# A two-batch channel attention with a SiLU feed-forward on one core: one fixed instruction order from the second pair on, the transposed attention in the scores' PSUM bank, other gaps for v's splits

## Chip, cores and metric

The kernel runs on 1 core of one Trainium2 chip. The metric is device time in microseconds (us). Three runs of the kernel before gave 1025.42, 1025.69 and 1026.45 us; the median is 1025.69 us.

## The reference

Two batches of 6016 positions and 256 channels go through an attention between channels, and its output, read as 12032 tokens of 256, through a feed-forward of width 2048.

```python
def _attn_ref(q, k, v, tau):
    qn = q / (np.linalg.norm(q, axis=1, keepdims=True) + 1e-06)
    kn = k / (np.linalg.norm(k, axis=1, keepdims=True) + 1e-06)
    s = kn.transpose(0, 2, 1) @ qn / tau          # 256 x 256 for each batch
    s = s - s.max(-1, keepdims=True)
    a = np.exp(s)
    a /= a.sum(-1, keepdims=True) + 1e-09
    return v @ a

def _moe_ref(x, w_in, w_out):
    h = x @ w_in                                  # 256 -> 2048
    g = h * (1.0 / (1.0 + np.exp(-h)))
    return g @ w_out                              # 2048 -> 256
```

## The kernel before, in words

The attention matrix of a batch is multiplied into `w_in` once (`mix`), so that the feed-forward reads v directly. Every f32 factor is split into two f16 halves ("high" by ScalarE, the remainder "low" by VectorE), and a product is three f16 matmuls. Both big products are arranged as 2 x 2 block products with seven instead of eight multiplications; the sums and differences that this needs are made on VectorE, ScalarE and by accumulating DMAs.

**Pairs and units.** v's columns are cut into 12 pairs (0 to 11) of 1024 columns; pairs 5 and 11, the last of each batch, have 896. Pair 0 goes through `emit_pair_group`; pairs 1 to 11 through `emit_unit`, eight units (0 to 7) each. A full unit takes TensorE about 9.5 us. A unit has four gaps ("slots" 0 to 3), one after each yield of `emit_unit`; work of others is put into them:

- slot 0: the products `y`, `x`, `z` into the PSUM banks of those names; ScalarE copies y and x to `c` (L810, L812); VectorE makes `g<-c,z` (L790). VectorE also runs the remainder of the unit before (`hl<-g,sg,hl`, L803);
- slot 1: `y` and `x` again, ScalarE copies x (L821), VectorE `g<-c,y`, and the second remainder (L803) of the unit before;
- slot 2: `x` (S3 T3), VectorE `g<-x,c`;
- slot 3: `x` (A22 T4), ScalarE Silu `g<-x,alpha` (L793) straight from the bank. The next unit's second product writes this bank again.

The second layer's matmuls (`o<-...`, L913) stand in a list `ready` and fill each slot by a budget.

**v of the next pair** (`scale_v(p + 1)`). A generator scales v to its largest magnitude (four reductions L148 on VectorE, then `pow2_scale`, whose matmul goes through the bank `z`), and then writes the tile `m`: highs on ScalarE (L550, `m<-v_t` or `m<-x`), lows on VectorE (L553), and between them sums (L574, L559). For pair 1 alone the scale comes from a sum of squares on ScalarE. The table `V_PLACES` says in which unit and slot each step is taken; key 0 is for pair 4 and was the default, 1 for pair 5, 2 for pair 6.

**Attention of the second batch.** It is computed while pairs 0 to 4 run (`attention(1)`, its scores in the bank `a`), and ends at pair 5's start: the transposes `tp` (L411) go into the bank `z` (through `small_psum`), and `split` writes `aT` from there (L164 on ScalarE, L165 on VectorE), in two halves. From then on `mix(1, j)` for j = 0 to 7 makes the second batch's `wall` with twelve matmuls `w` each (L443, bank `a`), at the places that the table `MIXES` names by (pair - 4, unit, slot).

**Order.** Within pairs 1 to 11 TensorE, VectorE and ScalarE keep the order in which the program is written (`tc.manual_schedule`); this region is closed and opened again at each pair. Each engine works its list in order, so a waiting instruction holds what stands behind it.

Of the kernel before, what the change touches and what calls it, by code (L numbers as in the profile page):

```python
# [8 lines left out]
F16 = mybir.dt.float16  # L9
F32 = mybir.dt.float32  # L10
# [4 lines left out]
AF = mybir.ActivationFunctionType  # L15
ALU = mybir.AluOpType
AX = mybir.AxisListType
PSUM = bass.MemoryType.PSUM
P = 128
# [11 lines left out]
def channel_attention_then_silu_ffn(ctx, tc, kq, qT, kT, vT, tau, w_in, w_out, outT):  # L31
    nc = tc.nc
    B, N, _, C = kq.shape
    DFF = w_in.shape[1]
    KC = C // P
# [8 lines left out]
    vp = ctx.enter_context(tc.tile_pool(name="vp", bufs=2))  # L44
    hp = ctx.enter_context(tc.tile_pool(name="hp", bufs=1))
    sm = ctx.enter_context(tc.tile_pool(name="sm", bufs=2))
    ps_b = ctx.enter_context(tc.tile_pool(name="ps_b", bufs=1, space=PSUM))
    firsts = {}
# [43 lines left out]
    def small_psum(name):  # L92

        if early[0]:
            return ps_o.tile([P, 512], F32, tag="o", name=name)
        return firsts["z"] if firsts else ps_b.tile([P, 512], F32, tag="z", name=name)
# [175 lines left out]
    def attention(b):  # L272
# [11 lines left out]
        for g, (j, n) in enumerate(groups[min(b, 1)]):  # L284
            if b and g >= 10:
                load_qk(b, g + 3)
            t = staged.pop((b, g))
            if b == 0 and g < 2:
                nc.scalar.activation(out=acc[:, g : g + 1], in_=t[:, :1], func=AF.Square)
            elif b == 0:  # L290
                if j + n == J:
                    nc.vector.tensor_tensor(
                        out=acc[:, 0], in0=acc[:, 0], in1=acc[:, 1], op=ALU.add
                    )
                sq = st.tile([P, 2, 2, C], F32, tag="sq", name="sq", bufs=2)
                nc.scalar.activation(out=sq[:, :n], in_=t[:, :n], func=AF.Square)
                a = acc[:, g % 2 : g % 2 + 1] if g < 4 else acc[:, :n]
# [33 lines left out]
        else:  # L331
            half = sm.tile([P, 2 * KC], F32, tag="half", name="half", bufs=1)
            nc.vector.tensor_scalar(
                out=tot, in0=tot, scalar1=1e-30, scalar2=None, op0=ALU.add
            )
            nc.vector.tensor_scalar(
                out=half.bitcast(U32), in0=tot.bitcast(U32), scalar1=1, scalar2=None,
# [3 lines left out]
                out=half, in0=half, scalar1=SEED, scalar2=None, op0=ALU.mult  # L341
            )
            yield
            for _ in range(2):
# [4 lines left out]
                    out=half, in0=half, scalar1=0.5, scalar2=None, op0=ALU.mult  # L349
# [3 lines left out]
        if b == 0:  # L353
# [6 lines left out]
            out=rn, in0=rn, scalar=2e-6, in1=root, op0=ALU.add, op1=ALU.add  # L360
# [41 lines left out]

        aT = sm.tile([P, 2, KC, C], F16, tag="aT", name="aT", bufs=1)
        if b:
            tp = small_psum("tp")
            tps = [tp[:, cb * C : (cb + 1) * C] for cb in range(KC)]
        else:
            tps = [small_psum("tp")[:, :C] for cb in range(KC)]
        for cb, tp in enumerate(tps):
            for db in range(KC):  # L410
                nc.tensor.transpose(  # L411
                    tp[:, db * P : (db + 1) * P], es[cb][:, db * P : (db + 1) * P], ident
                )
        if b == 0:
            yield
        for cb, tp in enumerate(tps):
            src = tp.rearrange("p (d c) -> p d c", d=KC)
            split(src, *(aT[:, u, :, cb * P : (cb + 1) * P] for u in range(2)), 2.0**TOP)
# [78 lines left out]
    def scale_v(p):  # L497
        b, n, w = pairs[p]
# [24 lines left out]
            yield  # L523
        if p < 2:
            s, inv = yield from pow2_scale(amax, "v", bufs=2, square=p == 1)
        else:
            quarters = [x for kc in range(KC) for x in v[kc]]
            maxima = amax_of(quarters, "av")
            for _ in quarters:
                next(maxima)  # L530
                yield
            next(maxima)
            amax = steps(maxima)
            scale = pow2_scale(amax, "v", bufs=2)
            next(scale)
            yield
# [636 lines left out]
    with at(0):  # L1173
# [41 lines left out]
        next(sqgen)  # L1215
        filler = attention(1)
    V_PLACES = {
# [3 lines left out]
    }  # L1221
    MIXES = {
# [101 lines left out]
    turned_over = [mix(1, j) for j in range(NI)]  # L1324
    fixed = ExitStack()
    for p, (b, n, w) in enumerate(pairs):
        fixed.close()
        if p not in paired:
            firsts.clear()
        if p in paired:  # L1330
            fixed.enter_context(
                tc.manual_schedule(
                    engines={
                        mybir.EngineType.PE, mybir.EngineType.DVE, mybir.EngineType.Activation
                    }
                )
            )
# [3 lines left out]
        for i in range(NI):  # L1341
# [29 lines left out]
            for _ in (emit_unit if p in paired else emit_pair_group)(p, i):  # L1371
                if ahead:
                    behind(start, ahead, {mybir.EngineType.PE})
                    ahead = None
                if p == 0 and i < 2:
                    start = len(traced())
                    prepare()
                    behind(start, anchor, {mybir.EngineType.DVE, mybir.EngineType.Activation})
                take = 2 if p == 0 and i > 2 and len(pending) > 6 - slot else 1
                over = p == len(pairs) - 1 and i == NI - 1  # L1380
                held_over = p == closing and i == NI - 1
                room_left = 12 * take
                if p in paired:
                    room_left = (
                        (8, 12, 12, 0) if over else (8, 8, 12, 16) if held_over else
                        (8, 12, 12, 8) if p == 1 and i == 0 else (8, 12, 16, 8)
                    )[slot]
                queue = ready if p in paired else pending
                while queue and room_left > 0:
                    cost, run = queue.pop(0)  # L1390
                    run()
                    room_left -= cost
                mark()
                if p == 0 and i < NI - 1 and (i, slot) != (1, 1):
                    nextmix = background(nextmix)
                if p in paired:
                    for j in MIXES.get((p - closing, i, slot), ()) if closing else ():
                        background(turned_over[j])
                    places = V_PLACES.get(p - closing if closing else 0, V_PLACES[0])
                    vgen = background(vgen, places[i].count(slot))  # L1400
                elif i >= 1 and vgen is not None:
                    vgen = background(vgen, 2)
                if p == closing and (i, slot) == (3, 1):
                    steps(sqgen)
                    norms["go"] = True
                if filler is not None and b == 0 and (p or i >= 2):
                    if "go" not in norms or p != closing or slot in ATTENTION[i]:
                        filler = background(filler, 1)
                if p in paired and b == 0 and "go" not in norms and slot in SQUARES[i]:
                    sqgen = background(sqgen) or iter(())  # L1410
                if p == 0 and 2 <= i < 5 and slot in (0, 2):
                    wout = background(wout)
                if p == 0 and i >= 5:
                    if i == 5 and slot == 0:
                        wout = spend(wout, 100)
                        summing = prepare_sums()
                    summing = background(summing)
                slot += 1
# [42 lines left out]
```

## Time and profile before

| | |
|---|---|
| median of three runs | 1025.69 us |
| profiled execution, its own time | 1026.73 us |
| its span, first to last instruction | 1025.0 us |
| TensorE busy | 1006.4 us (98%) |
| VectorE busy | 850.5 us (83%) |
| ScalarE busy | 766.8 us (75%) |
| mean granted TensorE clock | 0.995 |

The profiled execution took 1.7 us more than its span and 1.0 us more than the median. In timeline rows the columns are start (us from the span's start), busy us, engine, source line, operation, written tile <- read tiles, shapes, count of merged instructions, and in brackets the idle time before the first of them with what ended it. Matmul ends are modelled.

### The profile page before, as it was taken

Reading aid. Unit: us, or ns where it says so; the run is one execution under the profiler, and the core shown is the slowest. Engines: PE = TensorE matmul, PEld = TensorE weight load, DVE = VectorE, ACT = ScalarE, POOL = GpSimd, SP = SyncE. Lnnn points to the kernel's source line nnn. Section 1 sums busy time; section 2 is a strip of 40 time slices with the busy share of each in tenths; the row PEclk is TensorE's granted clock in tenths of the full one; section 3 lists DMA queues with packets and bytes.
Section 4 is the critical chain, followed back from the end, with each engine's and each line's share of the span. In section 5 each row is a group of like instructions: output and inputs, shape, how many; then the busy total and the mean of one; then the engine's idle time right before and its main releaser. Section 6 shows DMA issues by size and latency. Waiting matters only on the chain.

```text
span 1025.0 us, 20950 instructions
## 1 busy us (share of the span) xinstructions
PE 1006.4 (98%) x8550; PEld 870.2 (85%) x8550; DVE 850.5 (83%) x1339; ACT 766.8 (75%) x1077; POOL 199.5 (19%) x283
## 2 busy tenths in 40 slices
PE   9999999999999999998999999999999999999997
PEld 8877545788888888887998988888888888889997
DVE  6997687688888888897889889889889888888776
ACT  6686797788887887877677867777777777677674
POOL 0011000122212222212122112212122122222231
PEclk9999999999999999999999999999999999999999
DMA  9996010546547547525335244444435435334343
GB/s 368 397 398 201 33 42 1 181 105 202 151 120 210 147 114 211 126 68 159 76 81 139 62 107 105 123 104 122 121 88 140 109 93 144 89 94 112 97 94 85
DMA packets 62036, 138.81 MB, mean 135 GB/s; under 512 B 6642, under 2 KB 20898, under 8 KB 61938
## 3 DMA queue, kind: packets, MB, share of 16 engines
q0 software_dynamic: 30672, 67.98, 28.5%
q1 hardware_dynamic: 30978, 68.95, 19.2%
q8 instruction: 67, 1.10, 0.5%
q10 hardware_dynamic: 288, 0.52, 0.1%
q14 instruction: 31, 0.25, 0.1%
HBM read 57.67 MB, written 12.32 MB: 68 GB/s over the span
## 4 chain that ended last, share of the span: by engine, by line
PE 72%; DVE 11%; ACT 10%; issue 3%; DMA 3%; DVEq 0%; POOL 0%; SPq 0%; ACTq 0%
PE o L913 32%; PE x L783 18%; PE y L783 9%; PE z L783 5%; PE sc L301 4%; ACT g L793 2%; DVE g L790 2%; DVE hl L803 2%; PE o L681 2%; ACT hl L800 2%; PE w L443 1%; DVE m L553 1%; DMA kq_t<-in_kq 1%; DMA raw<-in_w_in 1%; ACT g L729 1%
## 5 line engine op out<-in xcount | busy, mean ns | idle before, releaser
L783 PEld LDWEIGHTS <-wall 128*128 128x128 f16 x3696 | 361.0, 98 | 49.1 <-issue 12.1
L783 PE MATMUL x<-m,wall 128*128 128x256 f16 (+1 forms) x2112 | 283.9, 271 | 4.7 <-DVE g L790 2.2
L803 DVE SCALAR_TENSOR_TENSOR hl<-g,sg,hl 128x1024 f16<-128x1024 f32 (+1 forms) x176 | 221.2, 1257 | 69.3 <-ACT hl L800 68.5
L913 PE MATMUL o<-hl,wo 128*128 128x256 f16 (+1 forms) x2112 | 272.8, 271 | 0.7 <-DVE hl L803 0.7
L913 PEld LDWEIGHTS <-wo 128*128 128x128 f16 x2464 | 240.8, 98 | 24.2 <-issue 1.2
L793 ACT ACTIVATE g<-g,alpha 128x512 f32<-128x512 f32 (+3 forms) x176 | 160.7, 921 | 98.1 <-DVE g L790 97.2
L800 ACT ACTIVATE hl<-g,sg 128x1024 f16<-128x1024 f32 (+1 forms) x176 | 198.1, 1126 | 0.0
L1004 POOL DMA_DIRECT2D sums<-hl x109 | 97.3, 892 | 370.0 <-DMA sums<-hl 125.1
L783 PE MATMUL y<-m,wall 128*128 128x256 f16 (+1 forms) x1056 | 142.8, 272 | 0.1
L821 ACT COPY c<-x 128x512 f32<-128x512 f32 (+1 forms) x88 | 50.7, 577 | 77.4 <-PE x L783 77.2
L913 PE MATMUL o<-t,ws_lo 128*128 128x256 f16 (+1 forms) x398 | 95.3, 271 | 0.0
L913 PE MATMUL o<-t,ws_hi 128*128 128x256 f16 (+1 forms) x398 | 95.2, 271 | 0.0
L790 DVE TENSOR_TENSOR g<-x,c 128x512 f32<-128x512 f32 (+1 forms) x88 | 59.5, 676 | 28.6 <-PE x L783 28.4
L793 ACT ACTIVATE g<-x,alpha 128x512 f32<-128x512 f32 (+1 forms) x88 | 58.8, 668 | 27.0 <-PE x L783 26.4
L997 DVE TENSOR_TENSOR t<-t,hl 128x1024 f16<-128x1024 f16 (+1 forms) x111 | 75.2, 677 | 3.0
L913 PEld LDWEIGHTS <-ws_lo 128*128 128x128 f16 x704 | 69.0, 98 | 6.6
L913 PEld LDWEIGHTS <-ws_hi 128*128 128x128 f16 x704 | 69.0, 98 | 6.6
L301 PE MATMUL sc<-kq_t 128*128 128x256 f32 x320 | 73.8, 381 | 0.6 <-DMA kq_t<-in_kq 0.6
L997 DVE TENSOR_TENSOR t<-hl 128x1024 f16<-128x1024 f16 (+1 forms) x111 | 74.4, 670 | 0.0
L783 PE MATMUL z<-m,wall 128*128 128x256 f16 (+1 forms) x528 | 70.7, 270 | 3.2 <-DVE aT L165 3.2
L790 DVE TENSOR_TENSOR g<-c,y 128x512 f32<-128x512 f32 (+1 forms) x88 | 59.2, 673 | 17.3 <-ACT c L821 16.1
L1002 POOL DMA_DIRECT2D sums<-hl x44 | 31.1, 707 | 204.8 <-DVE hl L803 140.6
(194 smaller groups left out, 1344.1 us busy)
## 6 DMA issues: line engine op xcount, KB each, us to landing
sums<-hl POOLq DMA_DIRECT2D x142, 256.0 KB, 3.3
kq_t<-in_kq SPq DMA_DIRECT2D x39, 512.0 KB, 8.7
sums<-t POOLq DMA_DIRECT2D x54, 256.0 KB, 3.5
extra<-hl POOLq DMA_DIRECT2D x42, 256.0 KB, 3.5
v_t<-in_vT SPq DMA_DIRECT2D x10, 1024.0 KB, 5.5
outT<-sb SPq DMA_DIRECT2D x40, 256.0 KB, 3.6
turned<-in_qT SPq DMA_DIRECT2D x10, 512.0 KB, 6.3
turned<-in_kT SPq DMA_DIRECT2D x10, 512.0 KB, 6.4
```

Of the source, the lines that this page charges most:

```text
L301: nc.tensor.matmul(sc[:, cb, :], t[:, i, 0, cb * P : (cb + 1) * P], t[:, i, 1, :], start=(j + i == 0 and cb == 0), stop=(j + i == J - 1), ...
L681: nc.tensor.matmul(o[:, :h], a[:, f, ee], hl[:, m, :h], start=(c == 1 and i == 0), stop=(c == NF and i == 2),)
L783: nc.tensor.matmul(bank[:, k * wide : (k + 1) * wide], mixed[b, i][:, v, a - 1], m[:, c, x, at : at + wide], start=(first and j + k == 0), ...
L790: nc.vector.tensor_tensor(out=g, in0=a[:, :h], in1=c[:, :h], op=ALU.subtract)
L793: nc.scalar.activation(out=g, in_=src, func=AF.Silu, scale=alpha)
L800: nc.scalar.activation(out=hl[:, :, 0], in_=g, func=AF.Copy, scale=sg)
L803: nc.vector.scalar_tensor_tensor(out=hl[:, :, 1], in0=g, scalar=sg, in1=hl[:, :, 0], op0=ALU.mult, op1=ALU.subtract,)
L821: nc.scalar.copy(c2[:, :h], x[:, :h])
L913: nc.tensor.matmul(o[:, side * wide : (side + 1) * wide], a, x, start=(first and j == 0), stop=(last and j == len(these) - 1), skip_group_ ...
L997: nc.vector.tensor_tensor(out=o, in0=x, in1=y, op=ALU.add)
L1002: nc.gpsimd.dma_start(o, x)
L1004: nc.gpsimd.dma_start(o, y, accum_op=ALU.add)
```

## The change

1. `fixed`, the region of fixed order, is opened once at pair 1 and stays open to the end.
2. For the second batch the transposes `tp` go to a tile of the bank `a`; the step after them is a yield of its own in both batches, so both halves of `aT` are written later and together.
3. `V_PLACES` has new entries: for ordinary pairs the step "low of the first half" moves from unit 5, slot 0 to unit 4, slot 3, and the sum `x<-v_t` from unit 5, slot 1 to unit 5, slot 2; pairs 4, 5 and 6 have their own tables.
4. v of pair 6 (`b and not n`) is scaled by its sum of squares: two Square activations with accumulation on ScalarE and a few one-column VectorE operations in place of four reductions; the pair's `m` is made earlier, as a place for the squares.
5. `MIXES` starts the mixes of the second batch earlier, in unit 3 of pair 5.

```diff
@@ attention
         if b:
-            tp = small_psum("tp")
+            tp = ps_b.tile([P, 512], F32, tag="a", name="tp")
...
-        if b == 0:
-            yield
+        yield
         for cb, tp in enumerate(tps):
@@ scale_v
         if p < 2:
             s, inv = yield from pow2_scale(amax, "v", bufs=2, square=p == 1)
+        elif b and not n:
+            sums = sm.tile([P, KC], F32, tag="av", name="av")
+            m = vp.tile([P, 2, 7, 512], F16, tag="m", name="m")
+            sq = m.rearrange("p a b c -> p (a b c)").bitcast(F32)
+            for kc in range(KC):
+                nc.scalar.activation(
+                    out=sq[:, :w], in_=t[:, kc, :w], func=AF.Square,
+                    accum_out=sums[:, kc : kc + 1],
+                )
+                yield
+            amax = sm.tile([P, 1], F32, tag="av1", name="av1")
+            nc.vector.tensor_tensor(out=amax, in0=sums[:, :1], in1=sums[:, 1:], op=ALU.add)
+            scale = pow2_scale(amax, "v", bufs=2, square=True)
+            next(scale)
+            yield
@@ V_PLACES
-        1: ((2, 3), (0, 2), (2, 3), (0, 1, 2, 3), (0, 2), (2, 3), (0, 1, 2), (1,)),
+        1: ((2,), (2, 3), (0, 1, 2), (0, 2, 2, 2), (0, 0), (3,), (3,), (0, 2)),
@@ the loop over pairs
-        fixed.close()
-        if p not in paired:
-            firsts.clear()
-        if p in paired:
+        if p == 1:
             fixed.enter_context(
```

On ScalarE at the start of pair 5 (line 793 Silu, 550 high of v, 800 high of hl, 810 to 821 copies out of the banks, 164 aT; in the changed kernel the lines are 807, 564, 814, 824 to 835 and 164, and 530 is the Square), before:

```order
L793 ACTIVATE g<-g,alpha 128x512
L550 ACTIVATE m<-x,sv 128x448
L793 ACTIVATE g<-x,alpha 128x512
L800 ACTIVATE hl<-g,sg 128x2x512
L164 ACTIVATE aT<-z 128x2x128
L810 COPY c_5351<-y 128x448
L812 COPY c_5351<-x 128x448
L800 ACTIVATE hl<-g,sg 128x2x512
L164 ACTIVATE aT<-z 128x2x128
L821 COPY c_5394<-x 128x448
```

and in the changed kernel:

```order
L807 ACTIVATE g<-g,alpha 128x512
L807 ACTIVATE g<-x,alpha 128x512
L814 ACTIVATE hl<-g,sg 128x2x512
L564 ACTIVATE m<-x,sv 128x448
L824 COPY c_5336<-y 128x448
L826 COPY c_5336<-x 128x448
L814 ACTIVATE hl<-g,sg 128x2x512
L164 ACTIVATE aT<-tp 128x2x128 x2
L835 COPY c_5380<-x 128x448
L807 ACTIVATE g<-g,alpha 128x2x448
L807 ACTIVATE g<-g,alpha 128x448
L530 ACTIVATE m,av<-v_t 128x1024
```

The last high of pair 5's v went behind the Silu and the first high of hl; the two halves of aT went behind the second high of hl, and a Square came in.

On VectorE in pair 1 (and alike in pairs 2, 3, 4, 6, 7, 8, 9 and 10), from the end of unit 4 to slot 2 of unit 5, before:

```order
L997 TENSOR_TENSOR t_1906<-t_1905,hl 128x1024
L803 SCALAR_TENSOR_TENSOR hl<-g,sg,hl 128x2x512
L645 RECIPROCAL back<-sg 128x1
L646 TENSOR_SCALAR back<-back,iwo 128x1
L790 TENSOR_TENSOR g<-c_2047,z 128x512
L553 SCALAR_TENSOR_TENSOR m<-v_t,sv,m 128x1024
L803 SCALAR_TENSOR_TENSOR hl<-g,sg,hl 128x2x512
L790 TENSOR_TENSOR g<-c_2093,y 128x512
L962 SCALAR_TENSOR_TENSOR sb<-o,back,sb 128x256
L574 TENSOR_TENSOR x<-v_t 128x512
L790 TENSOR_TENSOR g<-x,c_2047 128x512
L997 TENSOR_TENSOR t_2032<-hl 128x1024
```

and in the changed kernel:

```order
L1011 TENSOR_TENSOR t_1906<-t_1905,hl 128x1024
L567 SCALAR_TENSOR_TENSOR m<-v_t,sv,m 128x1024
L817 SCALAR_TENSOR_TENSOR hl<-g,sg,hl 128x2x512
L659 RECIPROCAL back<-sg 128x1
L660 TENSOR_SCALAR back<-back,iwo 128x1
L804 TENSOR_TENSOR g<-c_2048,z 128x512
L817 SCALAR_TENSOR_TENSOR hl<-g,sg,hl 128x2x512
L804 TENSOR_TENSOR g<-c_2093,y 128x512
L976 SCALAR_TENSOR_TENSOR sb<-o,back,sb 128x256
L804 TENSOR_TENSOR g<-x,c_2048 128x512
```

The low of v's first half went ahead of the first remainder of hl, and the sum x<-v_t went behind `g<-x,c` and the two sums t.

On VectorE in unit 6 of pair 5, around `g<-x,c`, before:

```order
L553 SCALAR_TENSOR_TENSOR m<-x,sv,m 128x1024
L803 SCALAR_TENSOR_TENSOR hl<-g,sg,hl 128x2x448
L790 TENSOR_TENSOR g<-c_6177,y 128x448
L473 TENSOR_TENSOR wall<-x,wall 128x896
L559 TENSOR_TENSOR x<-x,v_t 128x512
L790 TENSOR_TENSOR g<-x,c_6114 128x448
L997 TENSOR_TENSOR t_6095<-hl 128x2x448
```

and in the changed kernel (the row ahead of these is the last of three x<-x of a mix, as before):

```order
L817 SCALAR_TENSOR_TENSOR hl<-g,sg,hl 128x2x448
L804 TENSOR_TENSOR g<-c_6166,y 128x448
L804 TENSOR_TENSOR g<-x,c_6104 128x448
L1011 TENSOR_TENSOR t_6085<-hl 128x2x448
L1011 TENSOR_TENSOR t_6085<-t_6085,hl 128x2x448
L1000 TENSOR_TENSOR sb<-sb 128x448
L472 TENSOR_TENSOR wall<-x,wall 128x896
```

A low of v, the remainder `wall` of a mix and a sum of v no longer stand ahead of `g<-x,c`. The list of GpSimd is the same in both kernels; on the SyncE queue one store of pair 5's output now stands ahead of the load of pair 7's v.

## Rows read from the trace of the kernel before

**Rows 1.** The page: busy us, share of the span, instructions of each engine.
```profile
PE 1006.4 (98%) x8550; PEld 870.2 (85%) x8550; DVE 850.5 (83%) x1339; ACT 766.8 (75%) x1077; POOL 199.5 (19%) x283
```

**Rows 2.** Windows: length, then busy us (instructions) of PE, PEld, DVE, ACT, POOL, PEclk, DMA.
```profile
250.00:300.00 50.00, 50.00 (x461) 44.82 (x460) 40.69 (x62) 41.50 (x61) 10.73 (x15) 1.00 0.60 173
...
485.00:490.00 5.00, 5.00 (x34) 4.03 (x34) 2.25 (x5) 0.53 (x1) 0.79 (x1) 0.66 0.31 54
...
550.00:555.00 5.00, 4.44 (x30) 3.81 (x29) 4.03 (x8) 4.39 (x8) 0.73 (x1) 0.66 0.86 277
```

**Rows 3.** Timeline of TensorE: pair 5, unit 0, and the first product of unit 1.
```profile
479.54 0.74 PE L783 MATMUL y<-m,wall 128*128 128x224 f16 x6
481.01 0.73 PE L783 MATMUL x<-m,wall 128*128 128x224 f16 x6 [0.74 <-ACT g L793]
484.96 0.73 PE L783 MATMUL z<-m,wall 128*128 128x224 f16 x6 [3.21 <-DVE aT L165]
...
494.30 0.74 PE L783 MATMUL y<-m,wall 128*128 128x224 f16 x6
```

**Rows 4.** Timeline of ScalarE, same place.
```profile
479.74 0.65 ACT L550 ACTIVATE m<-x,sv 128x448 f16<-128x448 f32 x1
480.30 0.67 ACT L793 ACTIVATE g<-x,alpha 128x512 f32<-128x512 f32 x1
480.87 1.14 ACT L800 ACTIVATE hl<-g,sg 128x1024 f16<-128x1024 f32 x1
```

**Rows 5.** Timeline of VectorE, same place.
```profile
480.42 0.69 DVE L553 SCALAR_TENSOR_TENSOR m<-x,sv,m 128x448 f16<-128x448 f32 x1 [2.45 <-ACT m L550]
...
482.04 1.28 DVE L803 SCALAR_TENSOR_TENSOR hl<-g,sg,hl 128x1024 f16<-128x1024 f32 x1 [0.74 <-ACT hl L800]
...
484.48 0.42 DVE L165 SCALAR_TENSOR_TENSOR aT<-z,aT 128x256 f16<-128x256 f32 x1 [0.83 <-ACT aT L164]
...
485.73 0.62 DVE L790 TENSOR_TENSOR g<-c,z 128x448 f32<-128x448 f32 x1 [0.82 <-PE z L783]
```

**Rows 6.** Timeline of TensorE in pair 1, unit 5, slot 2, to unit 6, slot 0.
```profile
229.09 1.04 PE L913 MATMUL o<-hl,wo 128*128 128x256 f16 x8
230.24 0.81 PE L783 MATMUL x<-m,wall 128*128 128x256 f16 x6
...
231.76 0.82 PE L783 MATMUL y<-m,wall 128*128 128x256 f16 x6
232.67 0.81 PE L783 MATMUL x<-m,wall 128*128 128x256 f16 x6
```

**Rows 7.** Timeline of VectorE in the same unit.
```profile
223.40 1.28 DVE L803 SCALAR_TENSOR_TENSOR hl<-g,sg,hl 128x1024 f16<-128x1024 f32 x1 [0.98 <-ACT hl L800]
...
225.51 1.28 DVE L553 SCALAR_TENSOR_TENSOR m<-v_t,sv,m 128x1024 f16<-128x1024 f32 x1
...
229.49 0.69 DVE L790 TENSOR_TENSOR g<-x,c 128x512 f32<-128x512 f32 x1
```

**Rows 8.** Timeline of ScalarE: the high whose low Rows 7 show at 225.51.
```profile
220.62 1.13 ACT L550 ACTIVATE m<-v_t,sv 128x1024 f16<-128x1024 f32 x1
```

**Rows 9.** Timeline of TensorE: the same product x in pairs 4 and 6.
```profile
458.36 0.82 PE L783 MATMUL x<-m,wall 128*128 128x256 f16 x6 [0.37 <-DVE g L790]
...
621.74 0.81 PE L783 MATMUL x<-m,wall 128*128 128x256 f16 x6 [0.40 <-DVE g L790]
```

**Rows 10.** Timeline of TensorE in pair 5, unit 6.
```profile
547.90 0.83 PE L913 MATMUL o<-hl,wo 128*128 128x224 f16 x7 [0.71 <-DVE hl L803]
...
550.56 1.02 PE L783 MATMUL x<-m,wall 128*128 128x224 f16 x6 [1.45 <-DVE g L790]
```

**Rows 11.** Timeline of VectorE in the same unit.
```profile
548.29 1.09 DVE L473 TENSOR_TENSOR wall<-x,wall 128x896 f16<-128x896 f32 x1
549.29 0.69 DVE L559 TENSOR_TENSOR x<-x,v_t 128x512 f32<-128x512 f32 x1
```

**Rows 12.** Line 266, the Squares of q and k: count, ns min/median/max, first and last start.
```profile
L266 ACT ACTIVATE sq<-turned x24: 934/1042/1049, 193.1 to 433.4; 128x1024 f32<-128x1024 f32 x20, 128x896 f32<-128x896 f32 x4
```

More of the change, by code (lines that the diff above doesn't have):

```diff
@@ L1398, in channel_attention_then_silu_ffn @@
                         background(turned_over[j])
-                    places = V_PLACES.get(p - closing if closing else 0, V_PLACES[0])
+                    places = V_PLACES.get(p - closing if closing else None, V_PLACES[None])
                     vgen = background(vgen, places[i].count(slot))
```

12 rows, old and new, of tables (MIXES, V_PLACES) are left out of this document.

## Prediction

> **What bounds the kernel now.** I read the page's busy shares first, then windows, then the timeline of TensorE for every start that comes late, and last the engines named in the brackets. TensorE is busy 98% of the span, the next engine 83% [rows 1]. From pair 1 on it hardly rests: 50.00 of 50.00 us in a stretch that also holds the step from pair 1 to pair 2, 461 matmuls, so 0.1085 us for 256 columns and by columns 0.095 us for 224 [rows 2]. The change neither adds nor removes a matmul, so it can give back only what TensorE loses by waiting, and a lower clock behind a wait. I count a loss as the start of a matmul minus the start of the row before it plus its matmuls' time. The reader is to see three kinds:
>
> (a) Pair 5, unit 0. y starts at 479.54 and should be issued by 480.11, x starts at 481.01: 0.90 lost. x should be issued by 481.58, z starts at 484.96: 3.38 lost [rows 3]. (A bracket shows 0.17 less than this, because matmul ends are modelled; I add 0.17 where I use a bracket alone.) Then the granted clock is 0.66 over 485 to 490 [rows 2]: of its two levels the lower, 1.2 GHz, for 5 x 0.34 / 0.5 = 3.4 us, which costs half of that, 1.7 us. Sum 6.0 us. As a test: from the y of unit 0 to the y of unit 1, 14.76 us [rows 3], stand 42 matmuls of 224 and 44 of 256 columns, 8.8 us of work; 6.0 are lost.
>
> (b) Pair 5, unit 6. Two waits for VectorE, 0.71 + 0.17 and 1.45 + 0.17 [rows 10], together 2.5, and behind them again 0.66 over 5 us [rows 2], 1.7 us. Sum 4.2 us.
>
> (c) One place in each ordinary pair. At the end of unit 5 x waits for VectorE's `g<-x,c`: 230.24 against 229.09 + 8 x 0.1085, 0.28 lost; then the next unit's x, 232.67 against 231.76 + 6 x 0.1085, 0.26 lost, because the Silu that frees its bank came late [rows 6]. Pairs 2, 3, 7, 8 and 9 repeat this pattern; pairs 4 and 6 lose 0.37 + 0.17 and 0.40 + 0.17 at the first x [rows 9] and, I take it, 0.26 at the second. 6 x 0.54 + 0.80 + 0.83 = 4.9 us. Pair 10 shows no such wait before the first x.
>
> Together 15.1 us; of the few us of other late starts the change touches none.
>
> **The change, part by part.**
>
> *The bank of tp.* z waits because tp lies in its bank until both halves of aT are read; VectorE's part alone came 0.83 late behind ScalarE [rows 3, 5]. In the bank `a` nobody needs it before the first mix, three units later. This removes the 3.38 us. What is late next is x, which waits for the Silu `g<-x`. The new order puts that ahead of the high of v, so it starts at 479.74 instead of 480.30 [rows 4]; x at 480.45, 0.34 late in place of 0.90.
>
> *The price on VectorE.* The high of v now stands behind the Silu and a high of hl: it starts near 479.74 + 0.57 + 1.05 = 481.4 (their busy times less 0.1 of overlap, [rows 4]) and ends at 482.0. VectorE's low waits for it as it did before (2.45 us idle, [rows 5]), now until 482.05. Queued behind it are hl 1.28, `g<-c,z` 0.62, aT twice 0.42, hl 1.28, `g<-c,y` 0.62 [rows 5], two pairs of one-column operations (0.6, my estimate) and `g<-x,c` (0.62), with the low 0.69 in all 6.6 us; neighbours overlap by 0.09 (548.29 + 1.09 against 549.29, [rows 11]), nine times, so VectorE is through at about 488.0. TensorE has 36 matmuls of each width, 7.3 us, and the 0.34 before it needs that: 487.2, so 0.8 lost. The Silu in front of the next unit's x then waits for that one and for the first Square (1.04 and a read-out, [rows 12]) and ends near 490.5; x could start at 490.0: 0.5 lost. With rounding of the overlaps I take 1.8 us of new loss. Bounds: 0.34 if VectorE is early by a microsecond, and 3.5 if each of the three waits is twice as long. (a) gives back 6.0 - 1.8 = 4.2 us.
>
> *The clock.* [rows 2, 3] show the lower level right behind waits of 0.90 and 3.38 us, [rows 2, 10] behind 0.88 and 1.62; behind a lone 0.54 at 458.36 [rows 9] no stretch I read shows it. I leave 0.8 and 0.5, below both, so I count no fall. The Trainium skill (TensorE: Matmul & The Clock Gate, "HAM oscillation — how this bites in real kernels") says that idle between bursts of matmuls takes the array to half clock. By that rule the waits that I leave could call it again, and the time would be that of the first rival.
>
> *The squares.* They take four reductions off VectorE in units 0 to 2 and put two Squares of 1.04 us on ScalarE; 24 such Squares already ran between Silus [rows 12]. The first is priced above; the second, in unit 1, lies in ScalarE's idle time ahead of a Silu that waits for x anyway. Cover gone, it costs at most its own 1.2 us.
>
> *Steps and mixes moved in pair 5.* In unit 6 a low of v (1.2 us with overlap, by the 1024-wide low of [rows 7]) no longer stands ahead of the hl that TensorE waited 0.88 for, and beside it a `wall` (1.00) and a sum (0.60) no longer ahead of `g<-x,c` [rows 11], which comes 2.8 us earlier where 1.62 were missing [rows 10]. Both waits go, 0.3 us to spare at each. The moved work lands behind `g<-x,c` in units 3, 4 and 6, some 2.9 us in one unit, where VectorE then starts the next remainder 1 to 2 us late and has caught up by the next `g<-x,c`; the mixes' 1.3 us on TensorE widen just those units. Price 0, bounds 0 and the old 4.2. The load of pair 7's v goes behind one store; nobody reads that v before unit 2 of pair 6.
>
> *Ordinary pairs.* The low (1.20) moves into the 0.98 us in which VectorE waited for ScalarE before hl [rows 7]. Its high ends at 220.62 + 1.13 = 221.75 [rows 8], VectorE is free at 223.40 - 0.98 = 222.42, so it does not wait; hl starts 0.3 later, and nothing on TensorE needs it in that slot. From there on VectorE is 1.2 - 0.3 = 0.9 early, and without the sum (0.6) `g<-x,c` at 229.49 could run 1.5 earlier, that is as soon as its product is there; 0.28 were missing. The sum lands behind it, in front of stores only. All 4.9 us come back; bounds 0 and 4.9.
>
> *One fixed order.* At the pairs' borders the lists stand as before, and TensorE does not wait there [rows 2]: 0 from both sides.
>
> Sum: 4.2 + 4.2 + 4.9 = 13.3 us. The profiled execution would take 1026.73 - 13.3 = 1013.4; it stands 1.04 above the median, so the median after is 1025.69 - 13.3 = **1012.4 us**.
>
> **The rivals.**
>
> 1. The clock falls once more in pair 5. For it: the waits that I leave stand 2 us apart. Against it: they are shorter than those that were followed by a fall. 1012.4 + 1.7 = 1014.1 us.
> 2. VectorE's queue in units 5 to 7 only moves: `wall`, three x and a sum now follow each other behind `g<-x,c`, and the next hl is late by more than TensorE's matmuls cover. Then (b) stays: 1012.4 + 4.2 = 1016.6 us.
> 3. The low ahead of hl gives the late start to hl and `g<-c,z`, and (c) stays: 1012.4 + 4.9 = 1017.3 us.
> 4. Slower. The low stands ahead of hl, so VectorE now stands still if ScalarE's high is late, with hl, `g<-c,z`, hl, `g<-c,y` and `g<-x,c` queued behind. It has waited 2.45 us for just such a high [rows 5]. A wait of that size in nine pairs puts `g<-x,c` 2.45 later than the 228.4 I expect, with its 0.7 at 231.5 against 229.96: 1.5 lost each, 13.9 in nine, and (c) is not gained: 1012.4 + 4.9 + 13.9 = 1031 us. It decides from the point where the high ends some 2.5 us later than in [rows 8]: then nine losses of 0.9 eat the other gains. Against it: 0.67 us to spare.
> 5. The change does not do what it says (another wait holds z, the lists were never what was late): 1025.7 us.
>
> **How the numbers follow.** Forecast 0.66, rival 1 0.13, rival 2 0.06, rival 3 0.06, rival 4 0.05, rival 5 0.04. Without any new loss the time would be 1025.69 - 15.1 = 1010.6; from there to rival 2 and a little beyond, 1010.5 to 1017.0, lie the forecast and the first two rivals, 0.85. A measurement of this kernel can tell about 0.2%, 2 us. Faster by more: the forecast and rivals 1 to 3, 0.91; same: rival 5, 0.04; slower: rival 4, 0.05.
>
> **What would show it.** In the profile after, z of pair 5's unit 0 follows x within 0.1 us; the window behind it has clock 1.00; TensorE waits there twice for `g<-x`, under 1 us each, once with VectorE's `g<-x,c` as releaser. In unit 6 of pair 5 no wait over 0.3 us stands, and the window has clock 1.00. In ordinary pairs the x at the end of unit 5 starts 0.87 us behind the hl row before it, and VectorE's low shows no wait for ScalarE. I would be wrong if a bracket on DVE names `ACT m` in nine pairs, if a window in pair 5 shows a clock under 1.00, or if z waits for aT still.

## The result and the profile after

The changed kernel takes 1015.43 us (median of four runs, 1014.95 to 1015.79), the kernel before in the same measurement 1026.07 us (four runs): the ratio is 0.9895, interval [0.9877, 0.9912]. That is faster, with the whole interval below 1, and inside the predicted range, but 3.0 us above the predicted 1012.4. The profiled execution of after takes 1014.95 us with a span of 1013.2, 11.8 less than before in both.

The page of after, busy us, share of the span and instructions of each engine (against [rows 1]):

```profile
PE 1000.4 (99%) x8550; PEld 868.8 (86%) x8550; DVE 848.9 (84%) x1337; ACT 769.0 (76%) x1081; POOL 199.5 (20%) x283
```

The matmuls are the same 8550. To see where the time went I sum TensorE's losses: for each matmul its start minus the start of the matmul before it, less the usual distance for the shape of the matmul before (0.109 us for 256 columns, 0.096 for 224). Work at the lower clock counts as a loss in this sum. By stretches, in us:

| | before | after | gained | predicted |
|---|---|---|---|---|
| (a) pair 5, unit 0 and the start of unit 1 (470 to 500 us) | 6.22 | 2.15 | 4.07 | 4.2 |
| (b) pair 5, units 6 and 7 (540 to 560) | 4.12 | 1.93 | 2.19 | 4.2 |
| (c) ordinary pairs (200 to 470 and 560 to 930) | 6.21 | 1.58 | 4.63 | 4.9 |
| everything else | 8.70 | 8.20 | 0.50 | 0 |
| sum | 25.25 | 13.86 | 11.39 | 13.3 |

So (a) and (c) came as computed; of (b) half is missing.

**(a)** Timeline of TensorE, pair 5, unit 0 to the second product of unit 1, after (answers to [rows 3]; between these rows the matmuls run on, with no start more than 0.11 us late):

```profile
477.66 0.73 PE L797 MATMUL x<-m,wall 128*128 128x224 f16 x6
478.23 0.74 PE L797 MATMUL z<-m,wall 128*128 128x224 f16 x6
...
483.06 0.73 PE L797 MATMUL x<-m,wall 128*128 128x224 f16 x6 [0.76 <-ACT c L835]
...
485.62 0.73 PE L797 MATMUL x<-m,wall 128*128 128x224 f16 x6
...
488.01 0.74 PE L797 MATMUL x<-m,wall 128*128 128x224 f16 x6 [0.22 <-ACT g L807]
```

z follows x after 0.57 us, its matmuls' own time: the 3.21 us for `aT` are gone. In exchange the x of slot 2 (S3 T3) waits 0.76 us for ScalarE's copy `c`. Why that copy is late shows the timeline of ScalarE there:

```profile
480.99 0.38 ACT L164 ACTIVATE aT<-tp 128x256 f16<-128x256 f32 x1
482.21 0.38 ACT L164 ACTIVATE aT<-tp 128x256 f16<-128x256 f32 x1 [0.83 <-DVE aT L165]
482.49 0.53 ACT L835 COPY c<-x 128x448 f32<-128x448 f32 x1
...
486.31 1.04 ACT L530 ACTIVATE m<-v_t 128x1024 f32<-128x1024 f32 x1
...
487.35 0.61 ACT L807 ACTIVATE g<-x,alpha 128x448 f32<-128x448 f32 x1
```

and the timeline of VectorE:

```profile
479.24 0.69 DVE L567 SCALAR_TENSOR_TENSOR m<-x,sv,m 128x448 f16<-128x448 f32 x1 [4.02 <-ACT m L564]
...
481.76 0.41 DVE L165 SCALAR_TENSOR_TENSOR aT<-tp,aT 128x256 f16<-128x256 f32 x1
482.62 0.42 DVE L165 SCALAR_TENSOR_TENSOR aT<-tp,aT 128x256 f16<-128x256 f32 x1 [0.45 <-ACT aT L164]
...
484.96 0.60 DVE L804 TENSOR_TENSOR g<-x,c 128x448 f32<-128x448 f32 x1
```

Both halves of `tp` lie in one bank, as they did in the kernel before, but now their two highs follow each other on ScalarE's list. ScalarE's high of the second half waits for VectorE's low of the first (0.83 us), and the copy stands behind it. That the bank they share makes this wait, and not the tile `aT` that both write, is borne out by the first batch, whose two halves have a bank each. There the second high does not wait for the first low (ScalarE and VectorE, before):

```profile
54.57 0.66 ACT L164 ACTIVATE aT<-tp 128x256 f16<-128x256 f32 x2 [0.37 <-PE tp L411]
...
55.70 0.74 DVE L165 SCALAR_TENSOR_TENSOR aT<-tp,aT 128x256 f16<-128x256 f32 x2
```

This agrees with the Trainium skill (PSUM — Partial Sum Buffer, "PSUM bank collisions raise a hardware error"), by which software must keep two engines apart by bank (strictly by bank and quadrant of partitions), not by address. The last two of the ScalarE rows of pair 5 show the price of the Square: it stands ahead of the Silu that frees the bank of the next unit's x, which starts 0.38 us late (0.22 in the bracket).

**(b)** TensorE at the end of unit 6 and the start of unit 7 in pair 5, after (answers to [rows 10]):

```profile
541.21 0.74 PE L797 MATMUL x<-m,wall 128*128 128x224 f16 x6
541.79 0.93 PE L927 MATMUL o<-hl,wo 128*128 128x224 f16 x8
542.56 0.74 PE L797 MATMUL y<-m,wall 128*128 128x224 f16 x6
545.08 0.74 PE L797 MATMUL x<-m,wall 128*128 128x224 f16 x6 [1.78 <-ACT g L807]
```

ScalarE there:

```profile
543.67 0.84 ACT L452 ACTIVATE x<-w,rows 128x256 f32<-128x256 f32 x2 [1.72 <-DVE wall L472]
544.39 0.63 ACT L807 ACTIVATE g<-x,alpha 128x448 f32<-128x448 f32 x1
```

VectorE there:

```profile
540.23 0.62 DVE L804 TENSOR_TENSOR g<-x,c 128x448 f32<-128x448 f32 x1
...
542.49 1.08 DVE L472 TENSOR_TENSOR wall<-x,wall 128x896 f16<-128x896 f32 x1
```

The two waits of [rows 10] are gone: nothing in unit 6 starts late. But 1.95 us are lost at the next unit's x. The mixes take turns in a buffer `x` that is two deep. The fourth mix's `x<-w` on ScalarE writes the buffer that the second mix's `wall` on VectorE still has to read. That `wall` now stands behind `g<-x,c` and three sums and ends at 543.57. ScalarE stands still from 541.95 to 543.67, and the Silu behind it, which has its product since about 541.9, runs at 544.39.

**The clock.** Windows: length, then busy us (instructions) of PE, PEld, DVE, ACT, POOL, PEclk, DMA (against the last two of [rows 2]):

```profile
485.00:490.00 5.00, 4.78 (x46) 4.27 (x45) 4.12 (x8) 5.00 (x9) 0.00 (x0) 1.00 0.02 4
540.00:545.00 5.00, 3.29 (x35) 3.13 (x33) 3.97 (x8) 2.94 (x6) 1.60 (x2) 1.00 0.68 174
545.00:550.00 5.00, 4.92 (x50) 4.78 (x50) 4.56 (x7) 4.55 (x8) 1.79 (x2) 1.00 0.50 132
```

The granted clock is 1.00 in pair 5, even behind the wait of 1.95 us.

**(c)** TensorE in pair 1 at the place of [rows 6], after:

```profile
228.51 1.04 PE L927 MATMUL o<-hl,wo 128*128 128x256 f16 x8
229.38 0.82 PE L797 MATMUL x<-m,wall 128*128 128x256 f16 x6
...
230.91 0.82 PE L797 MATMUL y<-m,wall 128*128 128x256 f16 x6
231.57 0.82 PE L797 MATMUL x<-m,wall 128*128 128x256 f16 x6
```

VectorE in the same unit (against [rows 7]):

```profile
221.76 1.28 DVE L567 SCALAR_TENSOR_TENSOR m<-v_t,sv,m 128x1024 f16<-128x1024 f32 x1
222.96 1.28 DVE L817 SCALAR_TENSOR_TENSOR hl<-g,sg,hl 128x1024 f16<-128x1024 f32 x1
...
227.84 0.69 DVE L804 TENSOR_TENSOR g<-x,c 128x512 f32<-128x512 f32 x1 [0.27 <-PE x L797]
```

Both late starts are gone: 0.87 us from the hl row to x (8 x 0.1085), 0.66 from y to x. VectorE's low finds its high done (it ended at 221.17 on ScalarE) and does not wait, and `g<-x,c` now waits for TensorE's product instead of the other way round.

### The profile page after: what moved, and what is told of

The parts are those of the page before. It is cut to its first block, busy times and chain, and to the rows that moved or that the text cites. A ratio compares the mean times of both kernels' runs of the same rounds, so it can differ in the third digit from the quotient of the medians.

```text
span 1013.2 us, 20954 instructions
## 1 busy us (share of the span) xinstructions
PE 1000.4 (99%) x8550; PEld 868.8 (86%) x8550; DVE 848.9 (84%) x1337; ACT 769.0 (76%) x1081; POOL 199.5 (20%) x283
## 4 chain that ended last, share of the span: by engine, by line
PE 80%; DVE 10%; ACT 5%; DMA 3%; issue 2%; DVEq 0%; POOL 0%; SPq 0%; ACTq 0%
PE o L927 37%; PE x L797 20%; PE y L797 10%; PE z L797 5%; PE sc L301 4%; PE o L695 2%; PE w L442 1%; DVE g L804 1%; DVE t L1011 1%; DVE hl L817 1%; DMA kq_t<-in_kq 1%; DMA raw<-in_w_in 1%; DVE hl L165 1%; ACT hl L164 1%; ACT g L743 1%
```

## Experiments

Theory: three gains that add up, less one new wait (ScalarE behind the moved `wall`). The experiments apply single parts of the change to the kernel before, then mend single places of the changed kernel. Losses by stretch, summed as above, for all profiled executions:

| | median us | (a) | (b) | (c) |
|---|---|---|---|---|
| before (profile shown) | 1025.69 | 6.22 | 4.12 | 6.21 |
| before again, one execution | 1025.29 | 6.14 | 3.17 | 6.21 |
| before, a third execution | 1026.48 | 6.22 | 4.12 | 6.21 |
| after | 1015.43 | 2.15 | 1.93 | 1.58 |
| bank alone | 1020.80 | 1.44 | 3.18 | 6.23 |
| ordinary pairs alone | 1021.78 | 6.22 | 4.01 | 1.57 |
| pair 5 alone | 1024.97 | 7.38 | 1.92 | 6.19 |
| after, fourth mix behind the Silu | 1013.16 | 2.15 | 0.15 | 1.57 |
| after, second half of aT behind the copy | 1014.18 | 1.28 | 1.94 | 1.57 |
| after, both moves | 1012.97 | 1.28 | 0.16 | 1.57 |
| after, order closed at each pair | 1015.38 | 1.80 | 1.94 | 1.57 |
| after, reductions for pair 6 | 1015.41 | 1.78 | 1.94 | 1.57 |

The first four experiments ran beside 15 runs of the kernel before with a median of 1025.52 us (1024.33 to 1027.29), the next four beside seven runs with 1026.03 (1024.82 to 1026.72).

### The bank of tp alone

```diff
@@ the kernel before, attention
-            tp = small_psum("tp")
+            tp = ps_b.tile([P, 512], F32, tag="a", name="tp")
...
-        if b == 0:
-            yield
+        yield
```

> The kernel before with only the transposes moved into the bank of the scores (and the yield behind them in both batches). Theory (z waited for aT, and the low clock came behind that wait): z of pair 5, unit 0 follows x at once, the clock stays 1.00 there, 3.38 + 1.7 us come back and VectorE and ScalarE return about 0.9 us of it in the next products of the unit: 4.2 us less than before, ratio 0.996. The 0.90 us ahead of x stays, and unit 6 of pair 5 still loses 4.2 us with its low clock. Rival (the clock does not depend on that wait): 3.4 us or less, with a window of clock 0.66 still near 485 us. Rival (z waits for something else): no difference.

Measured: 1020.80 us (1020.43 to 1021.05), ratio 0.9953 [0.9941, 0.9966]. z follows x at once, and the clock stays at 1.00 behind the 0.90 us that x still loses; (a) falls from 6.22 to 1.44, less than the 2.15 of the whole change. So the bank brings all of (a), and the other edits in this place (ScalarE's new order, the Square, the one fixed order) take 0.7 of it back. With the order closed at each pair (a) is 1.80, so half of the 0.7 is the fixed order (see that experiment). What I had not foreseen is in unit 6. Timeline of TensorE there, with the waits of [rows 10] unchanged:

```profile
542.48 0.83 PE L912 MATMUL o<-hl,wo 128*128 128x224 f16 x7 [0.71 <-DVE hl L802]
...
545.14 0.73 PE L782 MATMUL x<-m,wall 128*128 128x224 f16 x6 [1.45 <-DVE g L789]
...
547.77 0.73 PE L782 MATMUL x<-m,wall 128*128 128x224 f16 x6 [0.55 <-ACT g L792]
```

and the window:

```profile
545.00:550.00 5.00, 4.31 (x43) 4.12 (x43) 3.85 (x8) 4.81 (x9) 0.73 (x1) 1.00 0.85 299
```

The clock did not fall, and in place of the slow stretch there is a third wait, 0.55 us for the Silu. (b) is 3.18 instead of 4.12.

### The ordinary pairs alone

```diff
@@ the kernel before, V_PLACES
-        0: ((), (0, 2), (3,), (0, 2, 3), (0, 1, 2), (0, 1, 2), (2, 3), (0, 1, 2, 3)),
+        None: ((), (0, 2), (3,), (0, 2, 3), (0, 1, 2, 3), (2, 2), (2, 3), (0, 1, 2, 3)),
+        0: ((), (0, 2), (3,), (0, 2, 3), (0, 1, 2, 3), (2, 2), (2, 3), (0, 1, 3, 3)),
...
-        2: ((), (), (3,), (0, 1, 2, 3), (0, 0, 1, 2), (0, 1, 2), (2, 3), (0, 1, 2, 3)),
+        2: ((), (), (3,), (0, 1, 2, 3), (0, 0, 1, 2, 3), (2, 2), (2, 3), (0, 1, 2, 3)),
...
```

> The kernel before with only the gaps of v's steps in pairs 1 to 4 and 6 to 10 as in the changed kernel. Theory: the first x at the end of unit 5 and the x of unit 6's slot 0 wait no more, 9 pairs together 4.9 us less than before, ratio 0.995; nothing in pair 5 changes. Rival (the low ahead of hl hands the late start on): no difference.

Measured: 1021.78 us (1020.69 to 1022.38), ratio 0.9962 [0.9949, 0.9974]. (c) falls from 6.21 to 1.57, the value of the whole change, and (a) and (b) stay within 0.11. Rivals 3 and 4 of the prediction are out. The median fell by 3.74 us, 1.2 less than expected and 0.9 less than (c) gives. The mean granted clock, which is on record for every run, goes with this: its median is 0.995 in these five runs and 0.997 in the 15 beside them. At equal clock (0.994, 0.995, 0.996 and 0.997) the difference is 4.1 to 4.7 us. Why these runs have more of the lower clock is open. The rows of pair 5 show why the bank is a gain of its own: TensorE comes earlier, and z waits the longer for it:

```profile
477.64 0.73 PE L783 MATMUL x<-m,wall 128*128 128x224 f16 x6
482.14 0.79 PE L783 MATMUL z<-m,wall 128*128 128x224 f16 x6 [3.77 <-DVE aT L165]
```

### Pair 5's steps, mixes and squares alone

The changed kernel with the bank of `tp`, the ordinary pairs' tables and the closing of the order at each pair as before.

```diff
@@ the changed kernel
-            tp = ps_b.tile([P, 512], F32, tag="a", name="tp")
+            tp = small_psum("tp")
...
-        None: ((), (0, 2), (3,), (0, 2, 3), (0, 1, 2, 3), (2, 2), (2, 3), (0, 1, 2, 3)),
-        0: ((), (0, 2), (3,), (0, 2, 3), (0, 1, 2, 3), (2, 2), (2, 3), (0, 1, 3, 3)),
+        0: ((), (0, 2), (3,), (0, 2, 3), (0, 1, 2), (0, 1, 2), (2, 3), (0, 1, 2, 3)),
...
```

> The kernel before with only pair 5 changed: its gaps for v's steps, the squares in place of the reductions, and the earlier mixes. Theory (the two waits in unit 6 go, with the low clock behind them, and a new wait of about 1.95 us comes in unit 7, where ScalarE's activations of the fourth mix wait for VectorE's wall): 4.2 - 1.95 = 2.2 us less than before, ratio 0.998, clock 1.00 near 550 us, and still 0.66 near 487 us. Rival (the squares cost more in units 0 and 1 than the reductions did): no gain or a loss.

Measured: 1024.97 us (eleven runs, 1023.26 to 1026.00), ratio 0.9989 [0.9981, 0.9998]: a quarter of what (b) should bring. (b) itself fell from 4.12 to 1.92 in this trace, with the same 1.95 us at unit 7's x as in after. But (a) rose by 1.16, and the rows say how. TensorE at z, and the window behind it:

```profile
484.10 1.28 PE L798 MATMUL z<-m,wall 128*128 128x224 f16 x6 [3.20 <-DVE aT L165]
```

```profile
485.00:490.00 5.00, 5.00 (x28) 3.71 (x26) 2.14 (x5) 0.53 (x1) 0.00 (x0) 0.51 0.30 52
```

The wait is the old one, but in this execution the lower clock lasted 6.8 us (483.1 to 489.9) instead of 3.4. Against the execution of before without a fall in unit 6, (b) gives only 3.17 - 1.92 = 1.25. Both make the gain of this part alone smaller and its runs spread over 2.7 us. Only one of the eleven runs has a trace, but the granted clocks bear it out: the five runs at 0.997 took 1023.90 us on average, the eight runs of the kernel before at 0.997 1025.15, so at equal clock the gain is 1.25, as much as (b) gives.

The medians of the three parts alone fall by 4.72, 3.74 and 0.55 us, 9.0 together, where the whole change gives 10.6. Two of these kernels keep z's wait and the lower clock behind it; that this is all of the difference is not shown.

### The fourth mix behind the Silu

```diff
@@ the changed kernel, MIXES
-        (1, 6, 0): (1, 2, 3), (1, 6, 2): (1, 3), (1, 6, 3): (2, 3),
+        (1, 6, 0): (1, 2, 3), (1, 6, 2): (1,), (1, 6, 3): (3, 2, 3),
```

> The changed kernel with one step of the fourth mix (its two activations x<-w on ScalarE) moved from slot 2 to slot 3 of unit 6 in pair 5, that is from ahead of the Silu g<-x to behind it and behind the high of hl. Theory (those activations wait for VectorE's wall<-x, which still reads their buffer, and hold the Silu that frees the bank of x): the 1.95 us loss ahead of x in unit 7 goes, at most 0.3 us returns later, 1.7 us less than the changed kernel: 1013.7 us against 1015.4, ratio to the kernel before near 0.988. Rival (ScalarE is simply behind there, by the sum of its work): the Silu comes as late, and no more than 0.5 us is won.

Measured: 1013.16 us (four runs, 1012.89 to 1013.64; none of them overlaps those of after), ratio 0.9880 [0.9865, 0.9895]. TensorE:

```profile
542.66 0.74 PE L797 MATMUL y<-m,wall 128*128 128x224 f16 x6
543.24 0.74 PE L797 MATMUL x<-m,wall 128*128 128x224 f16 x6
```

ScalarE:

```profile
542.09 0.63 ACT L807 ACTIVATE g<-x,alpha 128x448 f32<-128x448 f32 x1
...
543.71 0.84 ACT L452 ACTIVATE x<-w,rows 128x256 f32<-128x256 f32 x2
```

`x<-w` starts at the same time as in after (543.71 against 543.67) and costs nothing; the Silu ahead of it runs 2.3 us earlier, and x follows y at once. (b) goes from 1.93 to 0.15. The wait's cause is shown: not the work that was moved, but what stood behind the instruction that had to wait for it.

### The second half of aT behind the copy

```diff
@@ the changed kernel, attention
             split(src, *(aT[:, u, :, cb * P : (cb + 1) * P] for u in range(2)), 2.0**TOP)
+            if b and cb == 0:
+                yield
         yield
```

> The changed kernel with one thing moved: a step is put between the two halves of aT of the second batch, so that ScalarE's second high of aT stands behind its copy c<-x of slot 1 of pair 5's unit 0. Theory: in the changed kernel that high waited 0.83 us for VectorE's low of the first half, the copy stood behind it, and the x of S3 T3 waited 0.76 for the copy (0.93 lost). With the copy ahead the copy starts at once, the x behind it loses under 0.2, and TensorE gets 0.8 us back: 1014.6 against 1015.4. Rival A: VectorE is what is late there, and the loss only moves to the next x that waits for g<-x,c: 1015.4. Rival B: the copy itself waits for the x it reads and the bracket named the wrong thing: 0.76 stays at the same place, 1015.4.

Measured: 1014.18 us (1013.87 to 1014.78), ratio 0.9888 [0.9873, 0.9903]. ScalarE:

```profile
481.40 0.54 ACT L837 COPY c<-x 128x448 f32<-128x448 f32 x1
482.36 0.38 ACT L164 ACTIVATE aT<-tp 128x256 f16<-128x256 f32 x1 [0.41 <-DVE aT L165]
```

The copy runs 1.1 us earlier, `aT` still waits for VectorE's low of the first half, now with nothing urgent behind it, and the x of slot 2 has no bracket any more. (a) falls by 0.87, as expected; the medians differ by 1.25, and the intervals of the two ratios overlap, so the size is read from the trace.

### Both moves

The edits of the two experiments above, together.

> The changed kernel with both moves: the fourth mix's second and third product in pair 5's unit 6 both behind the Silu, in slot 3, and the second half of aT behind the copy c<-x in unit 0. Theory: the two losses lie 60 us apart on different buffers and add up: 2.3 (as the first move alone gave) + 0.8 = 3.1 below the changed kernel, 1012.3. Rival: the second move gives nothing, 1013.2.

Measured: 1012.97 us (1012.00 to 1013.37), ratio 0.9874 [0.9860, 0.9889]. Both losses are gone in the trace ((a) 1.28, (b) 0.16), yet the time is only 0.2 below that of the first move alone, and its profiled span is 0.3 longer (1011.4 against 1011.1): the stretch before 200 us, which no edit touches, lost 8.51 instead of 8.06, and the end 0.57 instead of -0.10. So the second move's 0.87 is seen at its place and is too small to be told in the whole time. This version and the fourth one are faster than both kernels.

### The order closed at each pair

```diff
@@ the changed kernel, the loop over pairs
-        if p == 1:
+        fixed.close()
+        if p in paired:
```

> The changed kernel, but the region of fixed order is closed and opened again at each pair, as in the kernel before. Theory: the lists stand alike and TensorE does not wait at a pair's border, so no difference: 1015.4, within 0.5. Rival: closing the region lets work of the border be put elsewhere, and each of the ten borders loses 0.3 us or more: 1018.5.

Measured: 1015.38 us (1015.21 to 1015.59), ratio 0.9899 [0.9885, 0.9914]; all stretches as in after but for 0.35 less in (a). The lists of TensorE, ScalarE and GpSimd are the same as in after. On VectorE one instruction stands elsewhere, at the start of pair 5: the first remainder of hl runs ahead of v's last low.

```profile
478.72 1.28 DVE L817 SCALAR_TENSOR_TENSOR hl<-g,sg,hl 128x1024 f16<-128x1024 f32 x1 [3.47 <-ACT hl L814]
479.92 0.68 DVE L567 SCALAR_TENSOR_TENSOR m<-x,sv,m 128x448 f16<-128x448 f32 x1
```

In after the low stands first (479.24, the VectorE rows of (a)), waits 4.02 us for its high and holds this remainder until 480.03. VectorE's low of `aT` is then late, ScalarE's second high waits 0.83 instead of 0.49 us for it, and the x of slot 2 loses 0.93 instead of 0.58. So the one fixed order costs 0.35 us at this place and changes no list elsewhere; in the whole time the 0.35 can't be told.

### Reductions for pair 6

The two Squares give way to the four reductions, two of them in unit 0 of pair 5, two in unit 1.

```diff
@@ the changed kernel, scale_v and V_PLACES
-        elif b and not n:
...
-        1: ((2,), (2, 3), (0, 1, 2), (0, 2, 2, 2), (0, 0), (3,), (3,), (0, 2)),
+        1: ((2, 2), (2, 2, 3), (0, 1, 2), (0, 2, 2, 2), (0, 0), (3,), (3,), (0, 2)),
```

> The changed kernel with the four reductions in place of the two Squares for the scale of pair 6's v, at the places that pair 5 gave them in the kernel before (two in unit 0, two in unit 1). Theory: with two reductions (some 2.2 us) more in unit 0's VectorE queue, behind its lows of aT, g<-x,c and the remainders come later, and what the Square cost (0.38 lost at the next unit's x) is more than paid: 0.5 to 2.0 slower, 1016.0 to 1017.4. Rival: VectorE has the time, and with the Square no longer ahead of the Silu the 0.38 comes back: 1015.0.

Measured: 1015.41 us (1014.97 to 1015.68), ratio 0.9898 [0.9882, 0.9915]: neither what the theory nor what the rival said. Two places changed and cancel. Timeline of TensorE at unit 1's first x and at a later x:

```profile
487.80 0.74 PE L782 MATMUL x<-m,wall 128*128 128x224 f16 x6
...
503.39 0.73 PE L782 MATMUL x<-m,wall 128*128 128x224 f16 x6 [0.40 <-DVE g L789]
```

The 0.38 behind the Square is gone, and 0.56 come in behind VectorE's `g<-x,c` further on. The Squares are neither gain nor loss here.

### The kernel before, twice more

> The kernel before, unchanged, as another profiled execution. Question: is the lower clock behind the waits of pair 5 (unit 0: 0.90 and 3.38; unit 6: 0.88 and 1.62) bound to these waits, or does it differ from one execution to the next? Theory (differs): the waits stand within 0.1 us, but one of the two falls is missing or lasts other than 3.4 us, as in the kernel with the bank alone, which had the waits of unit 6 and no fall. Rival (bound to the waits): both falls, 3.4 us each, and a time within 0.5 us of 1026.7.

> The kernel before once more, for the same question: with a third execution the falls behind unit 0 and unit 6 are counted three times. Theory (differs): not the same falls in all three, and the profiled times differ by about half the difference in time at the lower clock. Rival: the same two stretches in all three.

Measured: 1025.29 and 1026.48 us. The waits of unit 0 and unit 6 have the same lengths, within 0.03 us, in all three executions. The windows behind the waits of unit 6, in the second execution and in the third:

```profile
550.00:555.00 5.00, 4.13 (x42) 3.96 (x42) 4.03 (x8) 4.64 (x9) 0.73 (x1) 1.00 0.84 283
```

```profile
550.00:555.00 5.00, 4.69 (x32) 4.04 (x32) 4.02 (x8) 4.65 (x9) 0.73 (x1) 0.66 0.84 282
```

In the second the clock did not fall in unit 6, and TensorE then has a third wait:

```profile
552.94 0.73 PE L783 MATMUL x<-m,wall 128*128 128x224 f16 x6 [0.55 <-ACT g L793]
```

The two executions with both falls take 1026.48 and 1026.73, the one with one fall 1025.29. The rival, falls bound to the waits, is out.

## Why the prediction was right, and where it was short

**The bank of tp: right.** z follows x at once and no clock falls. The step before it was right too: x loses 0.31 us for 0.34 predicted.

**The price on VectorE in unit 0: right in size, wrong in place.** I had 0.34 + 0.8 + 0.5; the rows give 0.31 at x, 0.93 at the x of slot 2, 0.13 at that of slot 3 and 0.38 at the next unit's, 1.75 in all for 1.8. That the sum fits so well is luck: the largest term, 0.93, comes from a wait that I did not have, and the one that I put at 0.8 is 0.13. I followed VectorE's list to `g<-x,c` and did not follow ScalarE's: its second high of `aT` shares the bank with VectorE's first low, and the copy that TensorE needs stands behind it. In the experiment that moves the copy ahead, most of this loss goes; 0.35 of it come from the one fixed order.

**The clock: right that no fall comes, wrong in its price.** I counted 1.7 us for the fall in unit 6. With the fall (b) loses 4.12, without it 3.17: it costs 0.95 net, because at full clock TensorE reaches the next x too early for its Silu and waits for that instead.

**Ordinary pairs: right.** 4.63 of 4.9, by the mechanism named, and shown by themselves in the second experiment. The late starts that I named sum to 4.6 in the trace of before, so all of them came back; the 4.9 had 0.26 for a second one in pair 4 that I had not read and that measures 0.14, and the others rounded up.

**Steps and mixes moved in pair 5: the step that failed.** "Price 0, bounds 0 and the old 4.2": the price was 1.95. I checked where the moved work lands on VectorE and on TensorE, and asked of `wall` only whether VectorE catches up. I did not ask who waits for `wall`: ScalarE does, because the mixes' buffer is two deep, and on ScalarE's list the Silu stands behind that wait. Rival 2 had the place and a time near it, but named VectorE's `hl` as what comes late, which it does not. With the fourth mix behind the Silu the kernel takes 1013.16, 0.8 above the prediction.

**From the profiled execution to the median.** Measured trace against measured trace the shortfall is 1014.95 - 1013.4 = 1.5 us, the 1.95 and 0.4 more from (a) and (c), less 0.5 that came elsewhere and 0.4 that the sum of late starts does not hold. The other 1.5 of the 3.0 is this step: I took the gain, with both falls of the clock in it, from a profiled execution that stood 1.04 above its median, and subtracted it from the median. After's profiled execution stands 0.48 below its own. Both together are the 1.5. That the runs of the kernel before differ by the number of falls is seen in its three traces, with a mean granted clock of 0.995 for two falls and 0.997 for one (every trace here also has the lower clock at the very end of its span). The other runs have no trace, but their clocks go the same way: beside the first four experiments the eight runs at 0.997 took 1025.15 us on average, the seven at 0.993 to 0.996 1026.38. The median run, 1025.69, stands at 0.997.

**Rival 5 and the border of the pairs:** rival 5 is out. The fixed order was costed at nothing; by the experiment that closes it again it costs 0.35 us, in pair 5, because there VectorE's low stands ahead of a remainder that could run.

## What to carry to other kernels

When an instruction is moved later on one engine, look for who waits for its reads as well as its writes (a buffer two deep is such a wait), and then for what stands behind that waiter on its own list: here 1.95 us were lost by a Silu that needed neither. The mend here was to move the waiter behind the urgent instruction, not to move the work back. A gain that includes a clock fall can be worth less than the slow stretch shows (here 0.95 us in place of 1.7), and is to be taken from several executions, not from one.

## What the runs showed of the hardware

The lower clock behind the same waits is not the same in each execution. Behind unit 6's 0.87 and 1.62 us it came in three of five traces (before twice, the ordinary pairs alone) and not in two (before once, the bank alone). Behind z's wait of 3.4 to 3.9 us it came in all five traces that have that wait, for 3.4 us in four and for 6.8 in one (pair 5 alone). Behind the single wait of 1.95 us it came in none of five (after, pair 5 alone, the copy moved, the order closed, the reductions). The Trainium skill (TensorE: Matmul & The Clock Gate, "HAM oscillation — how this bites in real kernels") speaks of idle between bursts that takes the array to half clock; the traces agree for z's wait, and for unit 6 they agree in some executions only. What decides there is open.

With it goes the spread of the times: kernels that keep z's wait spread over 1.7 to 3.0 us (before 1024.33 to 1027.29, the ordinary pairs alone 1020.69 to 1022.38, pair 5 alone 1023.26 to 1026.00), those without it over 0.4 to 1.4 (after 1014.95 to 1015.79, the bank alone 1020.43 to 1021.05). The former have more runs (15, 5 and 11 against four or five), so part of this can be the count; but their mean granted clocks differ from run to run as well (0.993 to 0.997), and those of the latter less (0.998 to 1.000).
